# Expert weights from unit 23 on, x copies on ScalarE, and a new order of the last rows and scatters, in a kernel of attention and experts

## The chip, the core and the metric

The kernel runs on one core of a Trainium2 chip. TensorE multiplies matrices into PSUM; VectorE, ScalarE and GpSimd (POOL in the profile) do the elementwise work, each from a queue of its own in program order; SyncE (SP) and GpSimd issue the DMA transfers. The metric is device time in microseconds (us). Times are the median of the runs shown; a profile is one execution.

## The reference

Linear attention with cosine weights is followed by a layer of eight experts, in which each of 4608 tokens uses the one expert with its highest gate logit:

```python
q_p = phi(q, cos_w, sin_w); k_p = phi(k, cos_w, sin_w)     # relu(x)*cos, relu(x)*sin
kv = np.einsum('bhsf,bhsd->bhfd', k_p, v)                   # B=8, H=8, S=576, D=64
z = np.sum(k_p, axis=2)
num = np.einsum('bhsf,bhfd->bhsd', q_p, kv)
den = np.einsum('bhsf,bhf->bhs', q_p, z)[..., None] + 1e-06
x = (num / den) as [4608, 512]
e_idx = argmax(x @ w_gate)                                  # 8 experts
h = np.maximum(x[mask] @ w1[e], 0.0)                        # 512 -> 1024
out[mask] = gate_w[mask, None] * eom[mask, e, None] * (h @ w2[e])   # 1024 -> 512
```

## The kernel before

**Attention** runs over 36 units. A unit is one batch and two chunks of tokens, nine units make a group of two batches. In a unit TensorE multiplies q by kv (`q_mm`, L530), ScalarE and VectorE combine the sine and cosine halves into `u` (L535, L537; two buffers of two units each), and `q_out` divides by the denominator: GpSimd writes the rows in f16 into `xrows` (L556), the gate logits are summed on VectorE. At a group's end `route` finds expert and place of each token (VectorE, and a few matmuls for the ranks), and `scatter` (L658) writes the rows by indirect DMA into `xs`, sorted by expert. `xrows` has two buffers, so group 3's first row multiply waits for the scatters of group 1. The last group is routed in two parts, four chunks (3_0) and five (3_4).

**Experts** are put in order of their token counts; rank r's two weight halves go into `wt[:, r]`. `load_w(r, m)` issues one half from GpSimd, w1 for m = 0 (L237), w2 for m = 1 (L240), each read as 2 MB of fp32 and written as 1 MB of f16. The dictionary `wload` says after which unit, and in the second half after which tile, a load is issued. Each load adds to a semaphore, `wsem[r % 2]`; ranks above 1 wait on GpSimd for rank r - 2. The space of ranks 2 to 7 holds attention's buffers first.

**Tiles** of 128 tokens go through the experts, tile 0 to 38, with names by tile: `fetch(j)` reads 128 rows of `xs` into one of eight x buffers (SP, L794), `x_tr(j)` transposes them on TensorE (L804), a copy brings them from PSUM to `xts` (L820), `layer1(j)` is two groups of four matmuls (L852) and a ReLU on ScalarE into `hs` (L860), `h_tr(j)` transposes h, on TensorE up to tile 17 and from 37 on, by DMA for 18 to 36, and `layer2(j)` multiplies (L870), scales on VectorE (L877) and scatters the rows to the output from GpSimd (L881). The first eight tiles come from the tokens of groups 0 and 1 (`early_table`), the others from a table (`late_table`) that needs all groups' counts. The x copy is where a tile waits for its weights: for tiles 2 to 21 it loads the two semaphore counts from the table into registers, and its engine waits on `wsem`.

The order of all this is written out by hand: a loop over units, then the first three tiles one by one, then a loop over tiles 3 to 39. In that loop stand, for each j, `h_tr(j-1)`, `x_tr(j+1)`, `layer1(j)`, `layer2(j-1)` while h is transposed by TensorE, and `layer2(j-2)` with DMA transposes; at the change between the two, tile 19 has no layer 2 behind it. Generators (`route`, `late_table`) are advanced a step at a time by `step()` and `next`.

## Time and profile before

| | |
|---|---|
| time, median of 3 runs | 336.33 us (333.39 to 336.87) |
| the profiled execution | 336.46 us, span 334.8 us, mean granted clock 0.979 |
| TensorE matmuls busy | 286.1 us (85% of the span) |
| VectorE, ScalarE, GpSimd busy | 188.0 us, 156.4 us, 141.4 us (56%, 47%, 42%) |
| weight loads | 16 of 1024 KB, median 14.4 us from issue to landing |
| HBM | 67.61 MB read, 16.17 MB written, 250 GB/s over the span |

Times in the rows further down count from the span's start. Units 23 to 35 lie at about 114 to 155 us, tile 0 starts at 157, the last output is issued at 327.7. A row of the timeline gives the start, the duration, the engine, the line with the operation and its operands, and in brackets how long the engine had idled and what released it. "PEld" is TensorE's loading of weights, "PEclk" the granted share of its full clock. A DMA share over 1 means that transfers overlap on the engines.

### The profile page before, as it was taken

Reading aid. Unit: us, or ns where it says so; the run is one execution under the profiler, and the core shown is the slowest. Engines: PE = TensorE matmul, PEld = TensorE weight load, DVE = VectorE, ACT = ScalarE, POOL = GpSimd, SP = SyncE. Lnnn points to the kernel's source line nnn. Section 1 sums busy time; section 2 is a strip of 40 time slices with the busy share of each in tenths; the row PEclk is TensorE's granted clock in tenths of the full one; section 3 lists DMA queues with packets and bytes.
Section 4 is the critical chain, followed back from the end, with each engine's and each line's share of the span. In section 5 each row is a group of like instructions: output and inputs, shape, how many; then the busy total and the mean of one; then the engine's idle time right before and its main releaser. Section 6 shows DMA issues by size and latency. Waiting matters only on the chain. (4 is left out here: it accounts for less than half of the span.)

```text
span 334.8 us, 10160 instructions
## 1 busy us (share of the span) xinstructions
PE 286.1 (85%) x3624; PEld 178.9 (53%) x3624; DVE 188.0 (56%) x548; ACT 156.4 (47%) x320; POOL 141.4 (42%) x184
## 2 busy tenths in 40 slices
PE   7859889888886878796958979988999999999980
PEld 3548777676665657663424545544554445444530
DVE  7484557567878989896668544434433323322330
ACT  3456889888979869752302212221232232223210
POOL 8003334328842776586677534242221322232231
PEclk9998999999999999998979999999999999999997
DMA  7997688678874877999998899999947777776811
GB/s 242 341 388 257 217 245 289 218 221 263 279 254 101 279 214 138 235 233 228 236 223 229 145 237 251 231 244 268 267 123 175 182 181 182 174 166 165 175 46 45
DMA packets 58208, 71.87 MB, mean 215 GB/s; under 512 B 23406, under 2 KB 38318, under 8 KB 58160
## 3 DMA queue, kind: packets, MB, share of 16 engines
q1 hardware_dynamic: 40608, 40.17, 42.6%
q0 software_dynamic: 17552, 31.05, 41.1%
q8 instruction: 32, 0.52, 0.7%
q14 instruction: 16, 0.13, 0.1%
HBM read 67.61 MB, written 16.17 MB: 250 GB/s over the span
## 5 line engine op out<-in xcount | busy, mean ns | idle before, releaser
L860 ACT ACTIVATE hs<-hp 128x1024 f16<-128x1024 f32 x39 | 39.9, 1023 | 118.3 <-PE hp L852 118.3
L852 PE MATMUL hp<-wt,xts 128*128 x312 | 75.3, 385 | 3.1 <-DVE xts L820 1.9
L870 PE MATMUL yps<-wt,hts 128*128 x312 | 74.9, 384 | 3.0 <-DVE ysb L877 1.5
L877 DVE TENSOR_SCALAR ysb<-yps,xg 128x512 f32<-128x512 f32 x39 | 29.3, 751 | 82.4 <-PE yps L870 82.4
L881 POOL DMA_INDIRECT out_dram<-ysb,sidx x31 | 30.2, 974 | 84.0 <-DVE ysb L877 81.9
L530 PE MATMUL qo<-kvm,wt 64*64 64x162 f32 x1024 | 43.4, 306 | 12.6 <-DVE wt L537 5.5
L870 PEld LDWEIGHTS <-hts 128*128 128x128 f16 x312 | 30.8, 99 | 40.9 <-issue 3.6
L537 DVE SCALAR_TENSOR_TENSOR wt<-qo,sinq,wt 128x324 f32<-128x324 f32 x72 | 36.8, 549 | 21.9 <-ACT wt L535 17.3
L852 PEld LDWEIGHTS <-xts 128*128 128x128 f16 x312 | 29.4, 99 | 32.2 <-issue 3.1
L535 ACT ACTIVATE wt<-qo,cosq 128x324 f32<-128x324 f32 x72 | 35.9, 536 | 17.6 <-PE qo L530 17.4
L530 PEld LDWEIGHTS qo<-kvm,wt 64*64 64x64 f32 x1024 | 34.9, 134 | 17.1 <-DVE wt L537 8.0
L392 PE MATMUL kvp<-wt 64*64 64x132 f32 x1080 | 38.3, 278 | 5.1 <-ACT wt L349 2.6
L556 POOL TENSOR_TENSOR xr<-wt,rc 128x512 f16<-128x512 f32 x36 | 38.0, 1062 | 6.4 <-DMA xs<-xr,di@1_0_1857 5.4
L392 PEld LDWEIGHTS kvp<-wt 64*64 64x64 f32 x1080 | 29.9, 132 | 12.4 <-ACT wt L349 7.1
L349 ACT ACTIVATE wt<-wt,tanc 128x256 f32<-128x256 f32 x63 | 31.6, 513 | 0.2 <-DMA wt<-in_v_dram 0.2
L573 POOL TENSOR_TENSOR gl<-wt,rc 128x256 f32<-128x256 f32 x12 | 7.6, 631 | 51.1 <-DVE rc L548 39.0
L342 ACT ACTIVATE wt<-wt,cosc 128x256 f32<-128x256 f32 x54 | 28.0, 518 | 0.0
L506 PE MATMUL qtp<-ident,qr 128*128 128x128 f32 x128 | 21.2, 288 | 3.7 <-DVE qr L492 2.0
L820 DVE COPY xts<-xtsp 128x512 f16<-128x512 f16 x39 | 16.3, 419 | 14.3 <-PE xtsp L804 4.8
L509 ACT COPY wt<-qtp 128x512 f32<-128x512 f32 x32 | 18.9, 589 | 5.9 <-PE qtp L506 5.7
L492 DVE TENSOR_SCALAR qr<-wt 128x512 f32<-128x512 f32 x32 | 19.6, 615 | 0.5 <-PE qtp L506 0.5
L506 PEld LDWEIGHTS qtp<-ident,qr 128*128 128x128 f32 x128 | 14.0, 143 | 8.9 <-DVE qr L492 3.4
(275 smaller groups left out, 303.3 us busy)
## 6 DMA issues: line engine op xcount, KB each, us to landing
wt<-in_moe_w_dram POOLq DMA_DIRECT2D x16, 1024.0 KB, 14.4
wt<-in_k_dram SPq DMA_DIRECT2D x16, 576.0 KB, 5.9
wt<-in_v_dram SPq DMA_DIRECT2D x16, 576.0 KB, 5.6
wt<-in_q_dram SPq DMA_DIRECT2D x16, 576.0 KB, 7.1
xg<-xs SPq DMA_DIRECT2D x43, 129.0 KB, 3.3
xs<-zt SPq DMA_DIRECT2D x9, 129.0 KB, 5.8
out_dram<-ysb,sidx POOLq DMA_INDIRECT x31, 2.9
hts<-hs SPq DMA_TRANSPOSE x19, 3.7
```

Of the source, the lines that this page charges most:

```text
L349: d = ACT.activation(tvs[:, c, :, 1:65], vbuf[b % 2][:, :, c, :], AF.Copy, scale=tanc[:, c:c + 1])
L392: mm = PE.matmul(outs(i, mp), kcs[rows, m, c, :], mov, start=first, stop=(c == NCH - 1), skip_group_check=True)
L506: PE.transpose(toks(tp[:])[:, mh, :, l, :], qr[:, l, 2 * mh:2 * mh + 2, :].rearrange("p m d -> p (m d)"), ident[:])
L530: PE.matmul(qo[64 * l:64 * l + 64, 2 * mp + ih, 0:162], qT[r, hf, ih, l, :], kvms[b if c < 4 else b - 1 + l][r, n0:n0 + 2, :], start=True, ...
L535: d0 = ACT.activation(t, qo[:, :, 0:81], AF.Copy, scale=cosq[:, c:c + 1])
L537: d1 = DVE.scalar_tensor_tensor(u[:, h0:h0 + 4, :], qo[:, :, 81:162], sinq[:, c:c + 1], t, ALU.mult, ALU.add)
L556: GP.tensor_tensor(xrows[:, slot + x, 0:DM].bitcast(F16).rearrange("p (h d) -> p h d", d=D), u[:, 8 * x:8 * x + 8, 0:64], rc[:, 8 * x:8 * ...
L852: mm = PE.matmul(hp[:, fh * 512:fh * 512 + 512], xts[:, kc, :], wt[:, bass.ds(ev, 1), kc * F + fh * 512:kc * F + fh * 512 + 512], start=(k ...
L860: ACT.activation(hs[:], hp, AF.Relu)
L870: mm = PE.matmul(yp, hts[:, fc, :], wt[:, bass.ds(ev, 1), 4 * F + fc * DM:4 * F + fc * DM + DM], start=(fc == 0), stop=(fc == 7))
L877: DVE.tensor_scalar(ysb[:], yp, xg[:, DM + 2:DM + 4].bitcast(F32), None, ALU.mult)
L881: d = GP.indirect_dma_start(out=out[:, :], out_offset=bass.IndirectOffsetOnAxis(ap=idx, axis=0), in_=ysb[:], in_offset=None, bounds_check= ...
```

## The change

It has four parts.

1. The loads of ranks 0 to 3 are issued after units 23 to 32 where they were issued after units 25 to 34 and, for the last half, among the first tiles. Those of ranks 4 to 7 start after tile 4, one a tile, w1 before w2. w2 is read so that a partition holds eight neighbouring rows of it; to match, the ReLU that writes `hs` reads its PSUM input in steps of eight values.
2. The copy of x from PSUM, with its waits for weights and register loads, goes from VectorE to ScalarE, into `x_copy`, which stands behind the ReLU of the tile ahead. The x transposes and copies of tiles 0 and 1 go from unit 34 to unit 33.
3. The three last row multiplies go from GpSimd to VectorE.
4. All scatters of the last group stand ahead of the first output scatter; the late table is advanced by three steps at tiles 3 and 4, where it was two at tiles 3 to 5, and fetches 8 and 9 follow tile 4 instead of 5.

```diff
-                "o (c p) d2 -> p (o c) d2", p=128))
+                "o (p c) d2 -> p (o c) d2", p=128))
...
+            elif rows == "later":
+                q_gates(g, u, glog, xrows, slot, n)
+                q_sum()
+                return
...
+        def q_row(eng, u, rc, xrows, slot, x):
+            eng.tensor_tensor(
+                xrows[:, slot + x, 0:DM].bitcast(F16).rearrange("p (h d) -> p h d", d=D),
+                u[:, 8 * x:8 * x + 8, 0:64],
+                rc[:, 8 * x:8 * x + 8].unsqueeze(2).to_broadcast([P, H, D]), ALU.mult)
...
+        def x_copy(j):
+            xg = xgs[j]
+            xp16 = xpss.pop(j)
...
-                    tab[jj:jj + 1, 0:2], engines=(mybir.EngineType.DVE,),
+                    tab[jj:jj + 1, 0:2], engines=(mybir.EngineType.Activation,),
...
-                DVE.wait_ge(wsem[m], n)
+                ACT.wait_ge(wsem[m], n)
...
-            DVE.tensor_copy(xts[:].rearrange("p k t -> p (k t)"), xp16)
+            ACT.copy(xts[:].rearrange("p k t -> p (k t)"), xp16)
...
-            ACT.activation(hs[:], hp, AF.Relu)
+            ACT.activation(hs[:].rearrange("p (c q) -> p c q", c=8),
+                           hp.rearrange("p (q c) -> p c q", c=8), AF.Relu)
...
-        wload = {25: [(0, 0)], 26: [(0, 1)], 28: [(1, 0)], 29: [(1, 1)], 31: [(2, 0)],
-                 32: [(2, 1)], 34: [(3, 0)]}
+        wload = {23: [(0, 0)], 24: [(0, 1)], 25: [(1, 0)], 27: [(1, 1)], 28: [(2, 0)],
+                 30: [(2, 1)], 31: [(3, 0)], 32: [(3, 1)]}
...
-            if i == NU - 2:
+            if i == NU - 3:
                 x_tr(0)
+                x_copy(0)
                 x_tr(1)
+                x_copy(1)
...
-        wload = {3: [(4, 1)], 4: [(4, 0)], 5: [(5, 0)], 6: [(5, 1)], 7: [(6, 0)],
-                 8: [(6, 1)], 9: [(7, 0)], 11: [(7, 1)]}
+        wload = {4: [(4, 0)], 5: [(4, 1)], 6: [(5, 0)], 7: [(5, 1)],
+                 8: [(6, 0)], 9: [(6, 1)], 10: [(7, 0)], 11: [(7, 1)]}
...
-        q_out(*outs[0])
         layer1(0, pkv.tile([P, 2, 512], F32, name="hp0", tag="kvp"))
-        x_tr(2)
+        step()
         layer1(1)
         h_tr(0)
+        x_tr(2)
+        x_copy(2)
         next(first_half, None)
-        scatter(NG - 1, 0)
-        scatter(NG - 1, 1)
-        q_out(*outs[1])
-        load_w(3, 1)
+        for x in range(4):
+            scatter(NG - 1, x)
         layer1(2)
+        step()
+        for g, u, glog, xrows, slot, n in outs:
+            for x in range(n):
+                q_row(DVE, u, rcs[(g, slot)], xrows, slot, x)
+        step()
         h_tr(1)
         x_tr(3)
-        step()
+        step(2)
+        assert not pending
+        for x in range(4, GC):
+            scatter(NG - 1, x)
+        x_copy(3)
         layer2(0)
-        scatter(NG - 1, 2)
-        scatter(NG - 1, 3)
-        step(3)
         layer2(1)
-        step()
-        assert not pending
-        scatter(NG - 1, 4)
-        scatter(NG - 1, 5)
...
-            for _ in range(2 if j < 6 else 0):
+            for _ in range(3 if j < 5 else 0):
                 next(late, None)
             if j < NMAIN:
                 layer1(j)
-            for c in {3: (6, 7, 8)}.get(j, ()):
-                scatter(NG - 1, c)
-
+            if j + 1 < NMAIN:
+                x_copy(j + 1)
...
-            for jj in {5: [8, 9], 6: [10, 11]}.get(j, [j + 5]):
-                if 5 <= j and jj < NSLOT:
+            for jj in {4: [8, 9]}.get(j, [j + 5]):
+                if 4 <= j and jj < NSLOT:
```

On GpSimd the first two loads of the program stood here before, in units 25 to 28 (`xr_1611` are rows of group 2, `xr_2290` the first of group 3, `xs<-xr_978` the last scatter of group 1):

```order
L237 DMA wt<-in_moe_w_dram 128x4x1024
L658 DMA xs<-xr_978,di@1_0_1857 36992x516
L556 TENSOR_TENSOR xr_1611<-wt,rc_8_2275 128x512
L1172 ISA
L240 ISA
L240 DMA wt<-in_moe_w_dram 128x8x512
L556 TENSOR_TENSOR xr_2290<-wt,rc_0_2529 128x512 x2
```

In the change the loads (0, 0) and (0, 1) have gone out already, after units 23 and 24, and at this place stand the third and fourth (`xr_2300` are now the first rows of group 3):

```order
L237 DMA wt<-in_moe_w_dram 128x4x1024
L663 DMA xs<-xr_978,di@1_0_1857 36992x516
L566 TENSOR_TENSOR xr_1611<-wt,rc_8_2286 128x512
L1189 ISA
L240 ISA
L240 DMA wt<-in_moe_w_dram 128x4096
L566 TENSOR_TENSOR xr_2300<-wt,rc_0_2540 128x512 x2
```

So the rows read alike, but the last scatter of group 1 now has three loads ahead of it in the queue and not one.

On ScalarE, in unit 33 before: the copy of q's last part, an exponential of the routing, the evictions of units 34 and 35, and the ReLU of tile 0.

```order
L517 COPY qTt<-qtt_2827 128x4x64
L632 ACTIVATE den@3_0_2839<-den@3_0_2839 128x4
L535 ACTIVATE wt<-qo_0_2842,cosq 128x324
L535 ACTIVATE wt<-qo_1_2853,cosq 128x324
L535 ACTIVATE wt<-qo_0_2895,cosq 128x324
L535 ACTIVATE wt<-qo_1_2906,cosq 128x324
L860 ACTIVATE hs_2937<-hp_2927 128x1024
```

In the change the two x copies, which wait for the weights of ranks 0 and 1, stand ahead of these evictions:

```order
L517 COPY qTt<-qtt_2839 128x4x64
L830 COPY xts_2854<-xtsp_2847 128x512
L830 COPY xts_2863<-xtsp_2856 128x512
L637 ACTIVATE den@3_0_2871<-den@3_0_2871 128x4
L535 ACTIVATE wt<-qo_0_2874,cosq 128x324
L535 ACTIVATE wt<-qo_1_2885,cosq 128x324
L535 ACTIVATE wt<-qo_0_2904,cosq 128x324
L535 ACTIVATE wt<-qo_1_2915,cosq 128x324
L870 ACTIVATE hs_2942<-hp_2932 128x1024
```

Two rows have come in. In the loop over tiles ScalarE had one ReLU a tile and nothing else; in the change it has, from the ReLU of tile 19 on:

```order
L870 ACTIVATE hs_4610<-hp_4611 128x1024
L822 TENSOR_LOAD tab_135
L822 ISA x4
L830 COPY xts_4642<-xtsp_4596 128x512
L870 ACTIVATE hs_4672<-hp_4673 128x1024
L822 TENSOR_LOAD tab_135
L822 ISA x4
L830 COPY xts_4704<-xtsp_4658 128x512
L870 ACTIVATE hs_4747<-hp_4748 128x1024
L830 COPY xts_4760<-xtsp_4733 128x512
```

Behind each ReLU now follow the register loads (up to tile 21) and the x copy of the next tile.

## Rows read from the trace of the kernel before

**Rows 1.** timeline, tiles 16 and 17: start us, us, engine, line [idle <-releaser]

```profile
236.58 1.89 PE L852 MATMUL hp<-wt,xts 128*128 x8
...
238.56 1.02 ACT L860 ACTIVATE hs<-hp 128x1024 f16<-128x1024 f32 x1 [3.10 <-PE hp L852]
239.82 0.65 PEld L837 LDWEIGHTS <-hs 128*128 128x128 f16 x8
...
240.70 1.89 PE L852 MATMUL hp<-wt,xts 128*128 x8
240.90 0.68 DVE L839 COPY hts<-htsp 128x1024 f16<-128x1024 f16 x1
...
242.03 0.42 DVE L820 COPY xts<-xtsp 128x512 f16<-128x512 f16 x1 [0.45 <-DMA wt<-in_moe_w_dram]
```

**Rows 2.** timeline, POOL in units 23 to 32, then TensorE and VectorE before tile 0

```profile
118.47 1.07 POOL L556 TENSOR_TENSOR xr<-wt,rc 128x512 f16<-128x512 f32 x1
...
136.81 2.05 POOL L556 TENSOR_TENSOR xr<-wt,rc 128x512 f16<-128x512 f32 x2 [5.38 <-DMA xs<-xr,di@1_0_1857]
...
153.36 1.07 POOL L556 TENSOR_TENSOR xr<-wt,rc 128x512 f16<-128x512 f32 x1
...
153.83 1.33 PE L530 MATMUL qo<-kvm,qTt 64*64 64x162 f32 x32 [0.27 <-DVE wt L537]
...
156.48 0.75 DVE L820 COPY xts<-xtsp 128x512 f16<-128x512 f16 x2 [2.23 <-DMA wt<-in_moe_w_dram]
...
157.05 3.54 PE L852 MATMUL hp<-wt,xts 128*128 x8 [1.89 <-DVE xts L820]
```

**Rows 3.** timeline, late table on VectorE and start of tile 5

```profile
182.52 0.16 DVE L779 TENSOR_TENSOR tl@l<-tl@l,pin@l 128x8 f32<-128x8 f32 x1
...
184.14 0.16 DVE L725 CAST tab<-sel@l 128x3 int32<-128x3 f32 x1
...
184.75 1.89 PE L852 MATMUL hp<-wt,xts 128*128 x8
...
187.06 0.15 DVE L737 TENSOR_TENSOR tab<-cj@l,sel@l 128x1 int32<-128x1 f32 x1
```

**Rows 4.** windows of 5 us: PE, PEld, DVE, ACT, POOL busy, PEclk, DMA, GB/s

```profile
130.00:135.00 5.00, 4.34 (x112) 3.43 (x100) 4.72 (x18) 5.00 (x15) 1.43 (x2) 1.00 1.09 205
155.00:160.00 5.00, 3.11 (x16) 1.14 (x9) 3.02 (x8) 0.76 (x2) 2.30 (x3) 0.71 1.09 199
```

**Rows 5.** who waited for whom: us in total, times, longest us

```profile
PE xtsp L804 <- DMA xg<-xs: 4.0, 3, 1.9
```

**Rows 6.** timeline, x(8) and tile 7

```profile
194.93 0.40 PE L804 MATMUL xtsp<-ident,xg 128*128 128x128 f16 x4 [1.85 <-DMA xg<-xs]
...
195.72 1.89 PE L852 MATMUL hp<-wt,xts 128*128 x8 [0.40 <-issue]
```

**Rows 7.** who waited for whom, SP's DMA queue

```profile
SPq L794 <- DMA out_dram<-ysb,xg: 25.1, 5, 5.6
```

**Rows 8.** line 237, loads of w1: issue to landing

```profile
DMA to landing us min/median/max: 8.8/14.3/18.5
```

**Rows 9.** groups by line and shape: busy us, mean ns of one, idle before

```profile
L860 ACT ACTIVATE hs<-hp 128x1024 f16<-128x1024 f32 x39 | 39.9, 1023 | 118.3 <-PE hp L852 118.3
...
L509 ACT COPY wt<-qtp 128x512 f32<-128x512 f32 x32 | 18.9, 589 | 5.9 <-PE qtp L506 5.7
...
L580 DVE TENSOR_REDUCE glog<-gl 128x32 f32<-128x256 f32 x16 | 9.3, 584 | 1.4 <-POOL gl L573 1.2
...
L361 DVE TENSOR_TENSOR wt<-wt,tanc 128x384 f32<-128x384 f32 x5 | 2.5, 552 | 0.2 <-DMA wt<-in_v_dram 0.2
```

**Rows 10.** timeline, layer 2 behind tile 20, later a ReLU and the next load

```profile
252.90 1.89 PE L870 MATMUL yps<-wt,hts 128*128 x8 [0.56 <-DMA hts<-hs]
...
260.50 1.02 ACT L860 ACTIVATE hs<-hp 128x1024 f16<-128x1024 f32 x1 [2.65 <-PE hp L852]
...
262.15 1.45 PEld L852 LDWEIGHTS <-xts 128*128 128x128 f16 x8
```

More of the change, by code (lines that the diff above doesn't have):

```diff
@@ L541, in q_mm, with q_out @@
                         tc.add_to_no_dep_group("att", d.ins)
-        def q_out(g, u, glog, xrows, slot, n, between=None):
+        def q_out(g, u, glog, xrows, slot, n, between=None, rows=None):
             rc = wk.tile([P, 2 * H], F32, name=f"rc{g}_{slot}", tag="rc")
@@ L555, in q_out @@
                     between()
-                GP.tensor_tensor(
-                    xrows[:, slot + x, 0:DM].bitcast(F16).rearrange(
-                        "p (h d) -> p h d", d=D),
-                    u[:, 8 * x:8 * x + 8, 0:64],
-                    rc[:, 8 * x:8 * x + 8].unsqueeze(2).to_broadcast([P, H, D]),
-                    ALU.mult)
+                q_row(GP, u, rc, xrows, slot, x)
             if late:
@@ L781, in late_table @@
             yield from table("l", tabs[1], pin)
-        xgs, xtss, hss, htss, evr = {}, {}, {}, {}, {}
+        xgs, xpss, xtss, hss, htss, evr = {}, {}, {}, {}, {}, {}
         yps = []
@@ L805, in x_tr @@
                              xg[:, kc * 128:(kc + 1) * 128].bitcast(F16), ident16[:, :])
+            xpss[j] = xp16
+        def x_copy(j):
+            xg = xgs[j]
+            xp16 = xpss.pop(j)
             if j < 2:
@@ L967, in step @@
                         pending.remove(p)
-        wload = {25: [(0, 0)], 26: [(0, 1)], 28: [(1, 0)], 29: [(1, 1)], 31: [(2, 0)],
-                 32: [(2, 1)], 34: [(3, 0)]}
+        wload = {23: [(0, 0)], 24: [(0, 1)], 25: [(1, 0)], 27: [(1, 1)], 28: [(2, 0)],
+                 30: [(2, 1)], 31: [(3, 0)], 32: [(3, 1)]}
         nsc = {3: 1, 4: 1, 5: 1, 6: 1, 7: 1, 8: 1}
-        nsc2 = {3: 1, 4: 2, 5: 1, 6: 1, 7: 1}
+        nsc2 = {3: 1, 4: 2, 5: 1, 6: 2, 7: 1}
         outs = []
@@ L1038 @@
                 else:
-                    outs.append(out_args)
+                    q_out(*out_args, rows="later")
+                    outs.append(out_args[:-1])
             assert n < 8 or i == NU - 1 or g == 0 or scd == GC
@@ L1136 @@
             x_tr(NMAIN)
+            x_copy(NMAIN)
             x_tr(NMAIN + 1)
+            x_copy(NMAIN + 1)
             for j in range(NMAIN, NSLOT + 1):
@@ L1142 @@
                         x_tr(j + 1)
+                        x_copy(j + 1)
                 if j < NSLOT:
```

## The prediction

> **What bounds the kernel now.** I read two repeated tiles of the expert stage first, then the timeline of the hand-over from attention to experts (148 to 190 us), then the windows, then who waits on the DMA queues. The chain that ended last covers only the final 1.1 us, so the stages have to be read one by one.
>
> In the expert stage TensorE is full. Up to tile 17 (h transposed by TensorE) a tile takes 240.70 - 236.58 = 4.12 us [rows 1]: two runs of 8 matmuls and 12 transposes without a gap. Shared out by columns that is 1.74 us for a run, 0.43 for the 8 transposes of h and 0.22 for the 4 of x; with h transposed by DMA a tile should then take 3.7. What only frees VectorE changes none of these tiles. Time can be won in four places:
> - The hand-over. Unit 35's q matmuls start at 153.83 and last 1.33, but tile 0 starts only at 157.05: its x copy stands in VectorE's queue until, at 156.48, the weights of ranks 0 and 1 are there [rows 2]. From tile 0 to tile 5 it takes 184.75 - 157.05 = 27.70 us [rows 2, 3], six tiles' worth and more for five.
> [...]
> - Three waits of TensorE for fetched rows, 4.0 us in all [rows 5]. Each costs a restart too: x(8) is transposed at 194.93 and tile 7 starts 0.79 later [rows 6], 0.57 more than the transposes need. In all 4.0 + 3 x 0.57 = 5.7.
> - Behind these stands the DMA queue: its engines are full in 130 to 135 [rows 4], and SP waits 25.1 us for output scatters before it may fetch into the x buffers that they read [rows 7].
>
> **The change, part by part.** The sum is made against the profiled execution, 336.46 us, which is 0.13 above the median.
>
> *Weights.* The first load now follows the row multiply of unit 23, which ends at 118.47 + 1.07 = 119.5 [rows 2]; the second and third come about 121.9 and 127.3, the fourth about 131. A w1 load that finds the queue emptiest lands 8.8 us after its issue [rows 8]; loads then follow each other at 1.05 MB / 205 GB/s = 5.1 us [rows 4]. So they land near 128, 133, 140 (with the last q halves among them) and 146, some 4 us ahead of the x copies two units before 153.83. Beside that cover the w2 layout, with one long run a partition for eight, is worth 0 to either side.
>
> POOL pays for it. Group 3's first row multiply waits until group 1's last scatter, in the same queue, has landed: 136.81 before [rows 2]. Three loads now stand ahead of that scatter instead of one; I estimate 140.5, 3.7 later. POOL then runs the same work up to pair (31, 32), whose second row multiply ended at 153.36 + 1.07 = 154.4 [rows 2] and now ends at 158.1. Unit 35 writes the u that this multiply reads, so its combine starts at 158.1, and tile 1, which takes over unit 35's PSUM, at 158.7. Tile 0 needs neither: it starts at 153.83 + 1.33 = 155.2.
>
> *Hand-over*, walked with: run 1.74, h transposes 0.43, ReLU 1.02 (from 0.25 after its last matmul) and ScalarE copy 0.59 [rows 1, 9], a small VectorE operation 0.2 (nine in 182.52 to 184.30 [rows 3]), a row multiply on VectorE 0.7 (384 elements take 0.552 [rows 9]; bounds 0.55, and POOL's 1.07). Tile 1 ends at 160.4. Its ReLU stands ahead of the copy of x(2) on ScalarE, so tile 2 runs from 162.4 to 164.1. VectorE then has the ranks of the last five chunks, three row multiplies and hts(1), until 168.2; layer 2 of tile 1 follows to 170.0, and eight operations finish the routing at 169.9. Tile 3 starts at 170.7, tile 4 at 174.9, tile 5 at 179.1, against 184.75: **-5.6**. Bounds: -7.5, if the scatter lands no later than before, and -2.3, if the clock is low in two runs behind the gaps of 1.2 to 1.8 us that are left (2 x 1.65, from 3.54 against 1.89).
>
> *Late table and fetches.* Three steps each at tiles 3 and 4 end the table at 178.2; before, it ended at 187.06 + 0.15 [rows 3]. The nine scatters issue at 1.28 us each ahead of all outputs, 170.8 to 177. The output of tile 0, whose x buffer fetch 8 takes, issues at 177.4 and lands about 180.3; fetch 8 starts there, and x(8) is wanted near 187.4, 7.1 us later. Before, x(8) came 7.7 us after the table [rows 3, 6], so I take half of that wait's 2.4 us. Fetches 14 and 15 wait for outputs 6 and 7; these stand behind three and four second-half loads where they stood behind four and five, and the first half has landed long before: their 3.3 in full. Together **-4.5**, bounds 0 and -5.7.
>
> *x copies on ScalarE.* They stand behind the ReLU of the tile ahead. With DMA transposes a ReLU starts at 260.50 and the next tile's weights load at 262.15, 1.65 later [rows 10]; ReLU 1.02, copy about 0.5 behind it and 0.05 of signal make 1.57. It fits by 0.08. With TensorE transposes the ReLU ends at 239.58 and its transposes load at 239.82 [rows 1]: 0.19 to spare. Up to tile 21 the copy also loads registers; on VectorE the copy behind hts starts 242.03 - 240.90 = 1.13 after it [rows 1], and as hts itself lasts 0.68, the loads run beside it. Beside a ReLU of 1.02 they add 0.1, within the slack. The exception is tile 20: no layer 2 stands between tiles 19 and 20, so 0.25 + 1.13 + 0.55 + 0.15 = 2.1 us of ReLU, registers, copy and signals stand there in place of 0.22 of transposes, 1.9 more, of which the 0.56 that layer 2 waits behind tile 20 [rows 10] is covered: 1.3. With tiles 19 and 21: **+1.5**, bounds 0 and 2.
>
> *The strided ReLU.* Its input now steps by 8 values. No row shows such a read by ScalarE, so both ends: 0, if a value costs a step whatever its distance, and the nearest row, VectorE's sum over heads, read from SBUF in steps of 16 values: (584 - 160) / 256 = 1.66 ns a value [rows 9] against ScalarE's (1023 - 589) / 512 = 0.85 [rows 9]. At 1.66 a ReLU takes 1.86. I take 0: that row has another engine, another memory and a sum in it, and TensorE writes two columns to this memory (8 x 512 in 1.89 us, 0.46 ns each [rows 1]) in the time that ScalarE takes for one value.
>
> [...]
>
> Sum: 336.46 - 5.6 - 4.5 + 1.5 = 327.9.
>
> **The rivals.**
> *The strided ReLU is dear* (ends slower). What a ReLU takes above 1.02, e, exceeds a slack of 0.08 on some 17 tiles and of 0.19 on some 15. The gain of 8.6 is gone when 17 (e - 0.08) + 15 (e - 0.19) = 8.6, e = 0.40: a ReLU of 1.42 us decides. At 1.86 the kernel takes 327.9 + 17 x 0.76 + 15 x 0.65 = 350.6. For it: the row of 584 ns. Against: the reasons above.
> *The fetch waits stay*, as the DMA queue is the real limit: eight loads of 5.1 us still go out about one a tile, and an earlier tile 5 only waits longer. For it: full engines, SP's 25.1 us. Against: the first half's loads are out of the way by then. 336.46 - 5.6 + 1.5 = 332.4.
> *The early loads choke POOL and ScalarE.* If each load takes the 8.8 us of a lone one, group 1's scatter lands near 146 and the weights near 155. The x copies stand ahead of two units' evictions on ScalarE, which then wait for weights too; the pair's multiply is 9 us late and tile 1 starts at 164, not 158.7: 327.9 + 5.3 = 333.2. For it: 136.81 was such a wait already. Against: the rate in rows 4.
> *The hand-over takes back what the order gives*, by low clock and new gaps, with the fetch waits unchanged: 336.46 - 2.3 + 1.5 = 335.7.
>
> **How the numbers follow.** Forecast 0.53 (own range 322 to 332), fetch waits 0.18, choke 0.10, hand-over 0.06, dear ReLU 0.13. The time is the forecast's, 327.9. The range, 321.5 to 338, leaves out most of the dear ReLU (0.1) and a hand-over better than its bound. About 1% is what a measurement of this kernel can tell from no change: 333.0 to 339.7. Faster: 0.53, most of the 332.4 (0.12) and some of the choke (0.04), 0.69. Slower: the dear ReLU and a worse choke, 0.14. The same: 0.17.
>
> **What would show it.** Right: ReLUs of 1.02 us, tile 0 near 155 at full clock, tile 5 near 179, no DMA wait ahead of x(14) and x(15), a gap of about 2 us ahead of tile 20, tiles of 4.12 and 3.7 us. Wrong: a ReLU over 1.1; row multiplies of units 27 and 28 after 142; x copies on ScalarE that wait for weights; the DMA waits unchanged.

## The result, and the profile after

The changed kernel takes 339.76 us (median of 6 runs, 337.73 to 340.90) where the kernel before takes 336.36: a ratio of 1.0101, 95% interval 1.0059 to 1.0143. A second comparison, in another group of runs, gave 0.9957 (0.9910 to 1.0004). So it is no change, or 1% slower; the forecast was 327.9. Ratios here compare fast runs; the profiled executions of two runs further down, e11_spread and b3_spread_before, were slow ones, and nothing is read from them that a fast execution does not show too.

The profiled execution of after took 337.73 us (span 336.1), the fastest of its six and only 1.3 above that of before. But its last output is issued at 331.11 and the span ends 5.0 us later; in before these are 327.72 and 7.1. So the work ends 3.4 us later, and the tail behind it is 2.1 us shorter. (The medians also differ by 339.76 - 336.36 = 3.40; that is chance, as they include the tail.) Most of the tail is a closing instruction of GpSimd, DRAIN, here in before and in after (duration ns min/median/max; the longest is the one meant):

```profile
L1172 POOLq DRAIN  x3: 51/111/4482, 329.5 to 334.5; - x3
...
L1189 POOLq DRAIN  x3: 51/111/2730, 332.4 to 335.7; - x3
```

It takes 4.48 us in the three kernels here that read w2 in rows of one (before, b3 and b4, 17552 packets on the software DMA queue) and 2.64 to 2.85 in the other 17 traces (10384 packets). I take the w2 layout to be its cause; the three also have the late first-half loads, and no run separates the two. The forecast had 0 for this. So every ratio below to the kernel before, but for b3 and b4, probably contains these 2.1 us.

Because of the tail I compare by the starts of tiles (layer 1, from the timelines):

| place | before | after | change | forecast change |
|---|---|---|---|---|
| tile 0 | 157.05 | 157.18 | +0.1 | -1.9 |
| tile 3 | 175.27 | 174.58 | -0.7 | -4.6 |
| tile 5 | 184.75 | 184.02 | -0.7 | -5.6 |
| tile 18 | 244.82 | 244.70 | -0.1 | -10.1 |
| tile 21 | 254.85 | 258.20 | +3.4 | -8.6 |
| tile 38 | 317.57 | 320.97 | +3.4 | -8.6 |

Three stretches went wrong: the hand-over, the tiles up to 18, and tiles 19 to 21. From tile 21 on both kernels take 3.68 us a tile.

The groups by line of after (busy us, mean ns of one, idle before): the ReLU, now with strided input, the matmuls of layer 1, their weight loads, and the x copy.

```profile
L870 ACT ACTIVATE hs<-hp 128x1024 f16<-128x1024 f32 x39 | 39.9, 1024 | 100.3 <-PE hp L862 100.3
...
L862 PE MATMUL hp<-wt,xts 128*128 x312 | 75.0, 383 | 8.7 <-issue 4.8
...
L862 PEld LDWEIGHTS <-xts 128*128 128x128 f16 x312 | 29.9, 98 | 39.1 <-issue 7.6
...
L830 ACT COPY xts<-xtsp 128x512 f16<-128x512 f16 x39 | 22.7, 584 | 5.1 <-ACT hs L870 1.7
```

The ReLU takes 1024 ns where it took 1023 [rows 9]: the stride costs nothing. But layer 1 now idles, with "issue" as its releaser. Tiles 9 and 10 of after on the timeline:

```profile
203.53 1.89 PE L862 MATMUL hp<-wt,xts 128*128 x8 [0.16 <-issue]
...
205.46 1.02 ACT L870 ACTIVATE hs<-hp 128x1024 f16<-128x1024 f32 x1 [2.77 <-PE hp L862]
...
206.60 0.59 ACT L830 COPY xts<-xtsp 128x512 f16<-128x512 f16 x1
206.77 0.65 PEld L847 LDWEIGHTS <-hs 128*128 128x128 f16 x8
...
207.37 0.27 PEld L809 LDWEIGHTS <-xg 128*128 128x128 f16 x4
207.43 0.39 PE L809 MATMUL xtsp<-ident,xg 128*128 128x128 f16 x4
...
207.93 1.50 PEld L862 LDWEIGHTS <-xts 128*128 128x128 f16 x8 [0.29 <-issue]
208.04 1.89 PE L862 MATMUL hp<-wt,xts 128*128 x8 [0.22 <-issue]
```

A tile takes 208.04 - 203.53 = 4.51 us here, 4.45 in most; it was 4.12 [rows 1]. From the x transposes to layer 1 it takes 0.61 us. In before it took 0.22, from this row to the layer 1 at 240.70 [rows 1]:

```profile
240.48 0.39 PE L804 MATMUL xtsp<-ident,xg 128*128 128x128 f16 x4
```

Between the two stands the load of the register that picks the expert's weights. The trace lists it by its own line (duration ns min/median/max), on the queue that issues TensorE's weight loads:

```profile
L852 PEldq TENSOR_LOAD <-tab x39: 300/307/666, 156.0 to 320.0; - x39
L852 PEldq FUSED_REGOPS  x39: 151/151/165, 156.6 to 320.6; - x39
```

That is 0.46 us in each tile. In before it ran while matmuls were still being worked off, and so cost nothing.

The hand-over of after, on the timeline:

```profile
142.92 2.23 POOL L566 TENSOR_TENSOR xr<-wt,rc 128x512 f16<-128x512 f32 x2 [11.56 <-DVE rc L547]
...
155.47 1.33 PE L530 MATMUL qo<-kvm,qTt 64*64 64x162 f32 x32 [0.82 <-DVE wt L537]
...
157.18 1.89 PE L862 MATMUL hp<-wt,xts 128*128 x8 [0.38 <-issue]
...
165.85 1.90 DVE L566 TENSOR_TENSOR xr<-wt,rc 128x512 f16<-128x512 f32 x3
...
168.00 0.68 DVE L849 COPY hts<-htsp 128x1024 f16<-128x1024 f16 x1
...
169.94 0.73 DVE L888 TENSOR_SCALAR ysb<-yps,xg 128x512 f32<-128x512 f32 x1
170.02 0.96 POOL L663 DMA_INDIRECT xs<-xr,di@3_0_3024  x1 [2.04 <-DMA xs<-xr,di@2_0_2638]
170.72 2.79 PE L881 MATMUL yps<-wt,hts 128*128 x8 [2.73 <-DVE ysb L888]
...
174.58 2.08 PE L862 MATMUL hp<-wt,xts 128*128 x8
```

Group 3's first row multiply comes 6.1 us later than in [rows 2], unit 35's matmuls 1.6 later. Tile 0 runs at full clock (1.89, not 3.54; 1.00 granted in 157.0 to 159.2), so that part of the gain is there. Layer 2 of tile 1 then waits 2.73 us, though its hts is ready at 168.68: what it waits for is the scaling of tile 0 (169.94), which stands behind eight routing operations on VectorE. After the wait the clock is low, and the matmuls take 2.79 us. That is not new: in before they took 3.14 (first row). The second is the window of after (columns as in [rows 4]):

```profile
171.62 3.14 PE L870 MATMUL yps<-wt,hts 128*128 x8 [0.25 <-DVE ysb L877]
...
170.00:175.00 5.00, 4.28 (x22) 2.42 (x22) 2.02 (x4) 0.00 (x0) 3.10 (x4) 0.66 0.98 277
```

Tiles 19 to 21 of after:

```profile
250.67 1.02 ACT L870 ACTIVATE hs<-hp 128x1024 f16<-128x1024 f32 x1 [2.07 <-PE hp L862]
252.11 0.59 ACT L830 COPY xts<-xtsp 128x512 f16<-128x512 f16 x1 [0.41 <-ACT hs L870]
252.84 2.98 PE L862 MATMUL hp<-wt,xts 128*128 x8 [1.98 <-ACT xts L830]
...
255.61 2.53 PE L881 MATMUL yps<-wt,hts 128*128 x8
```

The copy of x(20) stands behind the ReLU of tile 19, and no layer 2 lies between to cover it. Tile 20 waits 1.98 us, as forecast; behind the wait layer 1 takes 2.98 us and layer 2 2.53, where 1.89 is usual (granted clock 0.64 in 254 to 258). That low clock was not in the sum.

### The profile page after: what moved, and what is told of

Read it like the earlier page. It is cut to its first block, busy times and chain, and to the rows that moved or that the text cites. A ratio compares the mean times of both kernels' runs of the same rounds, so it can differ in the third digit from the quotient of the medians.

```text
span 336.1 us, 10138 instructions
## 1 busy us (share of the span) xinstructions
PE 288.5 (86%) x3624; PEld 181.4 (54%) x3624; DVE 175.1 (52%) x512; ACT 177.6 (53%) x359; POOL 135.8 (40%) x181
## 3 DMA queue, kind: packets, MB, share of 16 engines
q0 software_dynamic: 10384, 31.05, 38.0%
## 5 line engine op out<-in xcount | busy, mean ns | idle before, releaser
L870 ACT ACTIVATE hs<-hp 128x1024 f16<-128x1024 f32 x39 | 39.9, 1024 | 100.3 <-PE hp L862 100.3
L392 PE MATMUL kvp<-wt 64*64 64x132 f32 x1080 | 39.1, 282 | 6.6 <-ACT wt L349 2.8
L566 POOL TENSOR_TENSOR xr<-wt,rc 128x512 f16<-128x512 f32 x33 | 34.9, 1067 | 12.5 <-DVE rc L547 11.6
L392 PEld LDWEIGHTS kvp<-wt 64*64 64x64 f32 x1080 | 30.6, 135 | 13.7 <-ACT wt L349 7.5
L830 ACT COPY xts<-xtsp 128x512 f16<-128x512 f16 x39 | 22.7, 584 | 5.1 <-ACT hs L870 1.7
```

Of the source, the lines that this page charges most:

```text
L392: mm = PE.matmul(outs(i, mp), kcs[rows, m, c, :], mov, start=first, stop=(c == NCH - 1), skip_group_check=True)
L566: eng.tensor_tensor(xrows[:, slot + x, 0:DM].bitcast(F16).rearrange("p (h d) -> p h d", d=D), u[:, 8 * x:8 * x + 8, 0:64], rc[:, 8 * x:8 * ...
L870: ACT.activation(hs[:].rearrange("p (c q) -> p c q", c=8), hp.rearrange("p (q c) -> p c q", c=8), AF.Relu)
```

## The experiments

All ratios are to the kernel before, run beside them on the same chip; the six groups (A is that of the result) ran on different chips or at different times, and times are compared within a group alone; the steps from tile to tile further down are set side by side across groups. In groups B, E and F the kernel before takes 344 us; no trace of it from there exists. In the traces of these groups, but for e3, ScalarE or VectorE waits at tiles 4 to 7 for something that the profile calls remote (the longest waits are 6.1 to 8.8 us, in e12 5.1), as in this row of the run e2_copy_ahead; shorter ones, up to 3.5 us, stand earlier in most of them, and in the other groups there is none:

```profile
188.60 0.59 ACT L830 COPY xts<-xtsp 128x512 f16<-128x512 f16 x1 [6.72 <-remote]
```

| group, time of before | run | ratio, 95% interval |
|---|---|---|
| B, 344.81 | e1_load_ahead | 0.9941 (0.9893 to 0.9990) |
| | e2_copy_ahead | 0.9900 (0.9830 to 0.9970) |
| | e3_copy_dve | 0.9993 (0.9940 to 1.0046) |
| | b1_loads_alone | 0.9914 (0.9875 to 0.9952) |
| C, 337.38 | a1_after (the changed kernel) | 0.9957 (0.9910 to 1.0004) |
| | e5_loads_behind | 0.9956 (0.9910 to 1.0001) |
| | e6_l2_early | 0.9929 (0.9881 to 0.9976) |
| | e7_all_three | 0.9842 (0.9785 to 0.9900) |
| D, 337.87 | e8_copy_l2 | 0.9853 (0.9808 to 0.9899) |
| | e9_second_early | 1.0024 (0.9976 to 1.0072) |
| | e10_hand_over | 1.0110 (1.0049 to 1.0171) |
| E, 343.98 | e11_spread | 1.0079 (1.0030 to 1.0128) |
| | e12_spread_hand | 1.0024 (0.9986 to 1.0062) |
| | b3_spread_before | 1.0247 (1.0177 to 1.0317) |
| | b4_copy_alone | 1.0194 (1.0156 to 1.0231) |
| F, 343.93 | e8b_copy_l2 | 0.9896 (0.9836 to 0.9956) |
| | e14_hand_over2 | 0.9788 (0.9739 to 0.9838) |
| | e13_some_spread | 0.9761 (0.9708 to 0.9813) |

Steps from one tile's layer 1 to the next, from the timelines, in us (sums where several):

| | before | after | e1 | e2 | e6 | e8 | e13 | b4 |
|---|---|---|---|---|---|---|---|---|
| tile 2 to 3 | 12.41 | 11.30 | 11.50 | 9.84 | 8.52 | 8.50 | 8.53 | 13.68 |
| a tile from 8 to 12, most | 4.12 | 4.45 | 4.12 | 4.12 | 4.45 | 4.12 | 4.12 | 4.45 |
| tile 13 to 14 | 6.05 | 5.00 | 5.32 | 6.07 | 7.50 | 7.82 | 4.12 | 4.50 |
| tile 18 to 21 | 10.03 | 13.50 | 11.93 | 9.31 | 11.86 | 9.31 | 9.31 | 11.28 |

### The x copies

**e1_load_ahead**, the register load ahead of both transposes:

```diff
+            if 3 < j < NMAIN:
+                evr[j] = PE.value_load(tcol(2, j), min_val=0, max_val=7)
             if j < NMAIN and j - 1 not in BY_DMA:
                 h_tr(j - 1)
```

> The changed kernel, in which TensorE loads the register that picks the expert ahead of the transposes of h and x of a step (tiles 4 to 38) and not between the x transposes and layer 1. Theory, register load: the x transposes now wait for the ScalarE copy of the tile before (one of two PSUM buffers), the register load stands in TensorE's queue behind that wait, and about 0.35 us of it lies open in each tile with TensorE transposes. Then these tiles go from 4.45 us to about 4.12, some 13 of them, 4 us in all: about 335.8, against 339.8 for the changed kernel. The long step at tile 20 stays. Rival, copy latency: layer 1 waits for the x copy or for PSUM itself. Then tiles stay at 4.4 to 4.5 and the time at 339.8.

Its timeline, x transposes and layer 1 (line 866 there):

```profile
207.03 0.58 ACT L830 COPY xts<-xtsp 128x512 f16<-128x512 f16 x1
...
207.86 0.27 PEld L809 LDWEIGHTS <-xg 128*128 128x128 f16 x4
...
208.08 1.45 PEld L866 LDWEIGHTS <-xts 128*128 128x128 f16 x8
208.14 1.89 PE L866 MATMUL hp<-wt,xts 128*128 x8
```

The x transposes still wait for the copy (it ends at 207.61), but layer 1 follows them by 0.23 us and most tiles are back at 4.12. Of the two theories the register load is right, the copy's latency is not.

**e2_copy_ahead**, the copy ahead of layer 1 and so of the ReLU:

```diff
                 x_tr(j + 1)
+                x_copy(j + 1)
...
                 layer1(j)
-            if j + 1 < NMAIN:
-                x_copy(j + 1)
```

> The changed kernel, in which the x copy of tile j+1 stays on ScalarE but stands right behind its transposes, ahead of layer 1 of tile j and so ahead of that tile's ReLU. Theory, place of the copy: the x transposes no longer wait for a copy that stands behind a ReLU; tiles with TensorE transposes come back to 4.12 us and the steps at tiles 20 and 21 to 2 and 4.4 us (they are 4.1 and 5.4). 13 x 0.33 + 3.1: about 332.5. Rival, ScalarE itself: register loads (about 1.1 us) and copy (0.58) do not end within the 1.9 us of layer 1, the ReLU starts late; tiles of 4.3 us or more and a time above 336.

```profile
254.69 1.89 PE L862 MATMUL hp<-wt,xts 128*128 x8
...
256.64 1.89 PE L862 MATMUL hp<-wt,xts 128*128 x8
...
260.32 1.89 PE L862 MATMUL hp<-wt,xts 128*128 x8
```

Tiles 19, 20 and 21: steps of 1.95 and 3.68. Tiles of 4.12 too, so the theory holds by its steps; the ScalarE rival falls. The ratio agrees within its interval with the 332.5 us that I expected (0.9885 of before), though x(14) waits again (a step of 6.07).

**e3_copy_dve**, the same, on VectorE:

```diff
-                ACT.wait_ge(wsem[m], n)
+                DVE.wait_ge(wsem[m], n)
...
-            ACT.copy(xts[:].rearrange("p k t -> p (k t)"), xp16)
+            DVE.tensor_copy(xts[:].rearrange("p k t -> p (k t)"), xp16)
```

> The changed kernel with the x copies, their register loads and weight waits back on VectorE, right behind the x transposes as before the change; all other parts of the change stay. Theory, the copy part is what cost the time: tiles of 4.12 us, no long step at tile 20, about 332.5, as with the copy ahead of the ReLU on ScalarE. Rival, the loss lies in the hand-over: little changes, 338 or more.

The tiles are right (4.12, no long step at tile 20), the ratio is not. Tile 0 starts at 165.69, in e2 at 162.73, but that is not the edit: this execution is already 3 us behind in attention (unit 28's q matmuls start at 135.4 and 132.4). What the edit made shows behind tile 2: the steps to tiles 3, 4 and 5 are 13.40, 6.65 and 5.59 us, in after 11.30, 4.73 and 4.71. Layer 2 of tile 1 waits 4.62 us for the scaling of tile 0, which now stands behind the copy of x(3) as well on VectorE. The run undid one cost and made another; it does not tell theory from rival.

**b4_copy_alone**, the kernel before with this part alone, from tile 4 on:

```diff
-                    tab[jj:jj + 1, 0:2], engines=(mybir.EngineType.DVE,),
+                    tab[jj:jj + 1, 0:2], engines=((mybir.EngineType.Activation if act else
+                                               mybir.EngineType.DVE),),
...
             if j < NMAIN:
                 layer1(j)
+            if j + 1 < NMAIN:
+                x_copy(j + 1)
```

> The kernel before with one part of the change alone: in the loop over tiles (tile 4 on) the x copy, with its register loads and weight waits, goes from VectorE to ScalarE and stands behind the ReLU of the tile ahead. Theory, this part is what cost: tiles with TensorE transposes 4.45 us, steps of 4.1 and 5.4 or 3.8 us at tiles 20 and 21 where 1.95 and 4.4 were, in part made up by shorter waits for x(14) and x(15): 1.5 to 5 us slower, 1.005 to 1.015. My prediction's term for it was 1.5 us, 1.004.

1.94% of 343.98 is 6.7 us (5.4 to 7.9 by the interval): the part by itself costs more than all of the change did, and more than the 1.5 to 5 that I expected. The ten tiles from 8 to 18 take 45.66 us, 4.5 more than ten of 4.12; but the kernel before has fetch waits there that are gone in b4, and takes 44.84 in its profiled execution, 42.30 in b1, which has its loads there. So the net is 0.8 or 3.4 us. Tiles 18 to 21 take 1.3 or 2.0 longer than in these two. The rest, 1.3 to 4.6 us, I cannot place, as no trace of before from that chip stands beside it.

### The hand-over

**b1_loads_alone**, the kernel before with the first-half loads, the w2 layout and the strided ReLU:

```diff
-        wload = {25: [(0, 0)], 26: [(0, 1)], 28: [(1, 0)], 29: [(1, 1)], 31: [(2, 0)],
-                 32: [(2, 1)], 34: [(3, 0)]}
+        wload = {23: [(0, 0)], 24: [(0, 1)], 25: [(1, 0)], 27: [(1, 1)], 28: [(2, 0)],
+                 30: [(2, 1)], 31: [(3, 0)], 32: [(3, 1)]}
...
```

> The kernel before with the weight loads of the change alone (ranks 0 to 3 after units 23 to 32, w2 read in rows of eight with the strided ReLU); the second half's loads, the x copies, rows and scatters as before. My prediction's reason: the weights are there in time, the x copy of tile 0 no longer waits 2.2 us, the first row multiply of group 3 comes at 140.5; tile 0 near 155.5, time about 333 to 335. Rival, POOL pays as much: the first row multiply of group 3 waits about 11 us, to 143, for scatters that stand behind three loads, units 34 and 35 come 1.7 us later, and what the x copy wins is lost: tile 0 near 157, time 336 to 338.

0.9% faster (3.0 us, 1.7 to 4.3), the 333 to 335 of my reason, although GpSimd's wait is as long as the rival said (11.38 us). But 2.1 us of that are the shorter tail, if the tail of before was 7.1 us in this group too. So what the early loads are worth by themselves is not shown.

**a1_after**, the changed kernel unchanged, as base of group C.

> The changed kernel itself, on the chip of the three runs beside it, so that each edit is compared on one chip. It stood at 1.010 of the kernel before; about the same ratio, 1.00 to 1.02, is expected, with tiles of 4.45 us and the steps of 4.1 and 5.4 us at tiles 20 and 21.

Its trace repeats that of after within 0.6 us at every tile.

**e5_loads_behind**, one load ahead of group 1's last scatter instead of three:

```diff
-        wload = {23: [(0, 0)], 24: [(0, 1)], 25: [(1, 0)], 27: [(1, 1)], 28: [(2, 0)],
+        wload = {23: [(0, 0)], 26: [(0, 1), (1, 0)], 27: [(1, 1)], 28: [(2, 0)],
...
```

> The changed kernel, in which only one load (rank 0, w1) stays ahead of the last scatter of group 1 on GpSimd; the next three follow behind it, after units 26 and 27, the rest as in the change. Theory, the hand-over gain was lost to loads that stand ahead of that scatter: the first row multiply of group 3 comes about 9 us earlier (wait of 11.6 us falls below 3), the pair (31, 32) 3 us earlier, units 34 and 35 1.7 us earlier, tile 0 at about 155.5 instead of 157.2; the time 1.5 to 2 us under the changed kernel's on the same chip. Rival, the weights are then late: the two x copies on ScalarE, ahead of the evictions of units 34 and 35, wait for rank 1, and tile 0 comes no earlier or later; the same time or up to 3 us more.

```profile
135.12 2.30 POOL L566 TENSOR_TENSOR xr<-wt,rc 128x512 f16<-128x512 f32 x2 [2.10 <-DVE rc L548]
...
152.64 1.07 ACT L830 COPY xts<-xtsp 128x512 f16<-128x512 f16 x2 [2.11 <-PE qo L530]
153.70 0.95 ACT L535 ACTIVATE wt<-qo,cosq 128x324 f32<-128x324 f32 x2
```

The row multiply comes 7.8 us earlier, as meant, and unit 34's matmuls at 151.28, not 153.32. But the two x copies stay at 152.64, and the evictions of unit 34 stand behind them: tile 0 starts at 157.32, and 156.82 in a1_after. The row names unit 34's matmuls as what the copy waited for, but the copy does not read them. The second half of rank 1, issued at 132.49, lands 20.0 us later, at 152.5, right ahead of the copies: the wait is that for the weights. The ratio is that of a1_after. The rival is right: with GpSimd on time the next thing late is the copy, which the change had put ahead of the evictions.

**e6_l2_early**, layer 2 and scaling of tile 0 ahead of the last routing steps, its output scatter left where it was:

```diff
         x_tr(3)
+        out0 = layer2(0)
         step(2)
...
         x_copy(3)
-        layer2(0)
+        layer2_out(*out0)
         layer2(1)
...
```

> The changed kernel, in which layer 2 of tile 0 and its scaling on VectorE stand ahead of the last two steps of the routing (its output scatter stays where it is). Theory: layer 2 of tile 1 waits 2.7 us, not for hts(1) but for the scaling of tile 0, which stands behind eight routing operations; with it ahead of them layer 2 of tile 1 starts 1.2 us earlier, the clock does not fall for it (0.9 us more), tile 3 comes 2 us earlier, the time is 1 to 2.5 us under the changed kernel's. Rival: the last scatters go out later by the time of the scaling and the fetches follow, or tile 3 waits for its x copy and weights; no gain.

```profile
168.12 0.74 DVE L888 TENSOR_SCALAR ysb<-yps,xg 128x512 f32<-128x512 f32 x1
...
168.91 1.89 PE L881 MATMUL yps<-wt,hts 128*128 x8 [1.42 <-DVE ysb L888]
...
171.31 1.89 PE L862 MATMUL hp<-wt,xts 128*128 x8
```

Tile 3 follows tile 2 by 8.52 us instead of 11.3, at full clock (1.00 granted in 165 to 175); my forecast had 8.3. The ratio moves by 0.28% only, less than its interval, since a wait for x(12) and a longer one for x(14) follow.

**e7_all_three**, e2, e5 and e6 together.

> The changed kernel with three edits: the x copy ahead of the ReLU on ScalarE, three loads behind the last scatter of group 1, and layer 2 of tile 0 ahead of the last routing steps. If the three reasons are right and add up: 6.4 + 1.8 + 2 = 10 us under the changed kernel's on the same chip, about 0.98 of the kernel before. If the DMA queue is the real limit, the earlier tiles wait for x(8) and the later ones, and the gain is that of the copy alone, 5 to 6.5 us.

1.15% under a1_after, 3.9 us: less than the copy alone promised. Up to tile 10 it gains 6 us on a1_after, and at tile 16 it is no earlier: between them the steps to tiles 12 to 15 take 9.5 us more than 4.12 each. What is gained early is waited for later.

### The loads of ranks 4 to 7

**e8_copy_l2**, e2 and e6.

> The changed kernel with the x copy ahead of the ReLU and layer 2 of tile 0 ahead of the last routing steps; loads as in the change. It is the base for the next two. Theory, the DMA stream of ranks 4 to 7 is the limit up to tile 16: tile 3 comes 2.8 us earlier and tiles take 4.12 us, but x(11) to x(15) then wait for the DMA queue some 8 us in all, so that tile 16 starts no earlier than in the changed kernel; what remains is the 3 us at tiles 20 and 21 and the two tiles behind tile 16: 0.985 to 0.99 of the kernel before. Rival: the three loads that stood behind the scatter in the kernel with all three edits caused those waits; without them here the waits are gone, and the ratio is 0.975.

```profile
219.28 0.57 POOL L240 DMA_DIRECT2D wt<-in_moe_w_dram  x1
220.16 1.02 POOL L897 DMA_INDIRECT out_dram<-ysb,sidx  x1 [0.30 <-issue]
222.84 1.00 POOL L897 DMA_INDIRECT out_dram<-ysb,sidx  x1 [1.67 <-DMA out_dram<-ysb,sidx]
225.17 0.22 DVE L834 COPY_PREDICATED_SCALAR sidx<-valid,xg 128x1 int32 x1 [2.00 <-DMA xg<-xs]
225.19 0.40 PE L809 MATMUL xtsp<-ident,xg 128*128 128x128 f16 x4 [2.97 <-DMA xg<-xs]
```

1.5% faster than before. x(14) waits 2.97 us; a fetch waits for the output scatter that frees its buffer, and the scatters stand among the loads in GpSimd's queue.

**e9_second_early**, the first load of rank 4 ahead of the last five scatters, the others earlier:

```diff
         for x in range(4):
             scatter(NG - 1, x)
+        load_w(4, 0)
...
+        wload = {3: [(4, 1)], 4: [(5, 0)], 5: [(5, 1)], 6: [(6, 0)],
+                 7: [(6, 1)], 8: [(7, 0)], 9: [(7, 1)]}
...
```

> The run before it, with the first load of rank 4 ahead of the last five scatters (near 172, where the DMA engines run empty until 187) and the others one tile earlier or more (one a tile from tile 3 to 9). Theory, the stream: it ends some 8 us earlier than 240, the waits of x(11) to x(15) shrink by 5 to 8 us, the time is 4 to 7 us under the run before it (0.965 to 0.975 of the kernel before). Rival: the scatters land 5 us later behind that load and x(8) is late by as much; the gain is lost, the same time.

```profile
174.25 0.79 POOL L237 DMA_DIRECT2D wt<-in_moe_w_dram  x1 [0.44 <-issue]
...
179.56 1.01 POOL L663 DMA_INDIRECT xs<-xr,di@3_4_3121  x1 [4.32 <-DMA xs<-xr,di@2_0_2638]
...
191.20 0.61 PE L809 MATMUL xtsp<-ident,xg 128*128 128x128 f16 x4 [2.25 <-DMA xg<-xs]
```

1.7% slower than e8. The first of the last five scatters waits 4.32 us behind the load, x(8) is late, and the steps to tiles 7 to 10 are 7.25, 8.40, 5.81 and 5.07 us. In e8 the first of these scatters waits 1.93 us. My theory fell, and worse than its rival had it: SP waits 36.1 us for output scatters, 25.7 in e8. I read from this that each load that goes out earlier also holds up output scatters, and with them fetches.

**e10_hand_over**, e9 with e5's loads and the x copies of tiles 0 and 1 behind unit 34's evictions:

```diff
-            if i == NU - 3:
+            if i == NU - 2:
                 x_tr(0)
...
```

> The run before it, with three of the first four loads behind the last scatter of group 1 and the x transposes and copies of tiles 0 and 1 back in unit 34, behind its evictions on ScalarE. Theory, the hand-over needs both: GpSimd no longer 8 us late, and evictions that do not stand behind x copies which wait for weights; tile 0 near 155 instead of 157, the time 1 to 2 us under the run before it. Rival: the weights of rank 1 land near 152 to 155 in both and set tile 0, and the DMA stream sets the tiles behind; no gain.

Tile 0 starts at 153.28 (157.41 in e9) and tile 6 4.1 us earlier. Of this 2.6 us are not the edit: unit 24's q matmuls, ahead of every edit, start at 112.3 and 114.9. From there to tile 0 it takes 41.0 us, in e9 42.5. In e12, e13 and e14, which have the same two edits, it takes 41.5 to 42.2; in after, a1, e1, e2, e6, e8, e8b and e9, which have neither, 42.5 to 46.3; in e5 and e7, with the loads alone, 43.0 and 41.8. So the two edits together gain, by an amount that varies between executions; that both are needed rests on the row of e5, where the copies wait for the weights, and e7 speaks against it. The end does not come earlier (1.0110): tiles 7, 8 and 11 to 14 wait 17 us in all.

**e11_spread**, e8 with the loads of ranks 4 to 7 one or two tiles apart, most of them two:

```diff
...
+        wload = {4: [(4, 0)], 6: [(4, 1)], 8: [(5, 0)], 10: [(5, 1)],
+                 11: [(6, 0)], 13: [(6, 1)], 15: [(7, 0)], 16: [(7, 1)]}
...
```

> The changed kernel with the x copy ahead of the ReLU and layer 2 of tile 0 ahead of the last routing steps (0.985 of the kernel before), and the loads of ranks 4 to 7 after tiles 4, 6, 8, 10, 11, 13, 15 and 16 where they stood after tiles 4 to 11. Theory: the fetch waits come from output scatters that stand behind weight loads in GpSimd's queue: a load takes 5.1 us, a tile 4.12, so with one load a tile the queue falls back until x(14) waits 3 to 4 us. With two tiles to most loads these waits are gone: 4 to 5 us under the 0.985, about 0.972. Rival, DMA bandwidth as such or late weights: the waits move to the x copies of tiles 16 to 22, no gain.

**e12_spread_hand**, the same with the hand-over edits of e10.

> The run before it with the two hand-over edits as well: three of the first four loads behind the last scatter of group 1, and the x transposes and copies of tiles 0 and 1 in unit 34 behind its evictions. In an earlier run these brought tiles 0 to 6 some 4 us forward, and the waits for fetched rows behind them took it back. Theory: with the loads spread the gain stays, 2 to 4 us under the run before it, 0.960 to 0.967. Rival: x(8) waits for the last scatters and the late table, whose time is set by the DMA queue, so tile 7 comes no earlier; the same as the run before it.

**b3_spread_before**, the kernel before with this `wload` alone.

> The kernel before, with nothing changed but when the loads of ranks 4 to 7 are issued: after tiles 4, 6, 8, 10, 11, 13, 15, 16, where they stood after tiles 3 to 11. Theory: the waits of TensorE for x(14) and x(15), 3.3 us, and half of that for x(8) come from loads ahead of the output scatters; without them 3 to 5 us less, 0.985 to 0.99. Rival: they come from SP's own order or the DMA engines' load, 1.00.

Both miss their forecasts, 0.972 and 0.960 to 0.967. In e12 every step from tile 8 to tile 18 is 4.12 us, and 3.68 and 1.95 follow: the fetch waits did come from the loads. But tile 21 then comes 12.6 us after tile 20. There, SP's h transposes and layer 2:

```profile
253.11 6.06 SPq L842 DMA_TRANSPOSE hts<-hs  x1
...
260.87 3.57 PE L881 MATMUL yps<-wt,hts 128*128 x8 [6.90 <-DMA hts<-hs]
```

The transposes by DMA, which begin with tile 18, run into the last loads (issued at 241.13 and 244.29): 6.06 us to issue where 1.26 is usual, and layer 2 waits 6.90. My theory did not have that, and its rival looked for it at the x copies. The kernel before with the same loads (b3) loses 2.5%, with the same long step between tiles 20 and 21; e11 has it too.

**e8b_copy_l2, e14_hand_over2, e13_some_spread**: e8 again; e8 with e10's hand-over edits; and that with the loads in between:

```diff
...
+        wload = {4: [(4, 0)], 5: [(4, 1)], 7: [(5, 0)], 8: [(5, 1)],
+                 9: [(6, 0)], 11: [(6, 1)], 12: [(7, 0)], 13: [(7, 1)]}
...
```

> The same kernel as e8_copy_l2 (x copy ahead of the ReLU, layer 2 of tile 0 ahead of the last routing steps), as base for the two beside it on one chip; 0.98 to 0.99 of the kernel before, with a step of 7 to 8 us at tile 14.

> That base with the two hand-over edits: three of the first four loads behind the last scatter of group 1, and the x transposes and copies of tiles 0 and 1 in unit 34 behind its evictions; second-half loads after tiles 4 to 11 as in the change. Theory: tile 16 is set by the stream of the second half's loads, about 50 us from its first load, which GpSimd issues behind the last scatters; all of it comes 3 to 4 us earlier, and so does tile 16; 3 us under the base. Rival: the stream and the fetches end at the same time as before, the earlier tiles only wait longer; the same as the base.

> The run before it, with the loads of ranks 4 to 7 after tiles 4, 5, 7, 8, 9, 11, 12 and 13, between the two orders that ran: one a tile (fetched rows wait 4 us at tile 14) and two tiles apart up to tile 16 (no wait there, but the DMA transposes of h behind tile 18 run into the last loads and lose 9 to 10 us). Theory: the last load lands near 244, just ahead of the first DMA transpose; most of the 4 us at tile 14 is gone: 2 to 3 us under the run before it. Rival: transposes and loads still meet, steps of 6 us or more at tiles 19 to 21; no gain or slower.

e14 is 1.1% under its base (0.9788 and 0.9896, the intervals just meet): tile 0 at 160.04 and 164.23, and the gain reaches the end. e13 has no wait at tile 14 (4.12, in e14 4.59) and none behind tile 18; 0.27% more, within the interval, where I had expected 2 to 3 us. Its ratio is the lowest of all, 2.4% under the kernel before.

## Why the prediction was wrong

Forecast and measured time are 11.9 us apart. By the table of tiles 4.9 of them arise up to tile 5, 5.1 more up to tile 18 and 2.0 up to tile 21. Three terms of the sum failed; a fourth, the w2 layout, was put at 0 and is followed by a tail 2.1 us shorter, which hides a part of the loss.

**The x copies, forecast +1.5.** This term failed most as far as single parts were run: alone, in the kernel before, it costs 6.7 us (b4). I measured the slack from the ReLU to the next weights load (0.08 and 0.19 us) and saw that the copy ends in time. I did not ask what stands in TensorE's queue behind an instruction that the copy makes wait. The x transposes of the next tile reuse one of two PSUM buffers and wait for it; behind them stands the register load, 0.46 us, which ran for nothing as long as nothing ahead of it waited. e1 shows that: 4.12 us with it moved. The exception, tile 20, was seen and sized at 1.3; the wait of 1.98 there is right, the low clock behind it (2.98 and 2.53 for 1.89) was left out, and 13.50 - 10.03 = 3.5 us came of it.

**The hand-over, forecast -5.6, measured -0.7.** Three terms. GpSimd: three loads hold the scatter until 142.9, not 140.5, and tile 0 comes at 157.18, not 155.2; in e5 the other order of loads alone did not bring it, as the x copies stood ahead of the evictions; with both edits (e10, e12 to e14) tile 0 comes earlier, though e7 came near that with the loads alone. Layer 2 of tile 1: I let it wait for hts(1) alone and wrote 168.2; it waits for the scaling of tile 0, which the change had put behind the routing, and starts at 170.72 at low clock, as it did in before. e6 shows 2.8 us for it. And the tiles from 3 on were longer by the register load.

**Fetch waits, forecast -4.5.** They are gone in after, but for nothing: tiles of 4.45 us leave the fetches more time. With an earlier tile 3 (e6) or tiles of 4.12 (e2, e8) x(14) waits again: its step takes 7.50, 6.07 and 7.82 us. So "the full 3.3" for x(14) and x(15) was wrong, and the rival "the fetch waits stay" had the cause right. It is not the DMA rate alone: the order of loads and output scatters in GpSimd's queue, which the fetches wait for, makes the wait, as e13 shows against e14 and e11. I had counted the loads ahead of an output scatter and not how far the queue falls behind at one load of 5.1 us (my estimate) a tile of 4.12; in after the eight loads land 5.6 to 7.1 us apart.

**What was right.** The strided ReLU is free: with a step of 8 values it takes 1024 ns in after, and 1023 ns without in before. Tile 0 runs at full clock (1.00 granted), the weights are there in time (the fourth load lands at 147.7, the copies of tiles 0 and 1 start at 152.73), tiles with DMA transposes take 3.68. The rival "dear ReLU" fell. "Choke" was half right: the scatter of group 1 landed at 142.9, between my 140.5 and its 146, but the x copies were not held up in after (tile 1 at 159.29, not 164). "The hand-over takes back what the order gives" came nearest to the time, 335.7, at a chance of 0.06, but that is luck: it keeps the fetch waits, which are gone in after; the low clock at 170.72 is there in before too (171.62; 0.66 granted in 170 to 175 in both); and the one at 252.84 comes of the x copies, not of the hand-over.

The terms were added as if each stood alone. They meet in GpSimd's queue, and a gain ahead of tile 14 is kept only where the loads leave room: 331.87 us (e8), 339.49 (e9) and 340.34 (e10) in one group are the same early tiles, or earlier ones, with other load orders. What stays open: what "remote" is, how b4's 6.7 us divide between the tiles and the hand-over, why attention takes 2 to 3 us more in one execution than in another of the same first half, and whether the w2 layout alone shortens the tail.

## What to carry to other kernels

Before an instruction is moved to an engine with room, look at who needs its output buffer back, and at what stands in that waiter's queue behind the wait: the register load there, 0.46 us, was hidden only while the queue ran ahead (0.22 us from the x transposes to layer 1 in before, 0.61 in after). Gains in two stages that share a queue need not add (tile 0 came 4.1 us earlier in e10 than in e9, at ratios of 1.0110 and 1.0024; in e14 the gain reached the end); where weight loads, scatters and the fetches that wait for those share one, size the spacing of the loads first (one a tile, x(14) waited 2.97 us in e8; with the last two at 241 and 244 us, layer 2 waited 6.90 us for a DMA transpose in e12), and the hand-over after that.
